# Powers of the table parameters as wide products and wide Exp steps, two parameter sets copied on chip, and new allowances for the virtual clock of an S4D and MLP-mixer kernel

## The chip, the cores and the metric

The kernel runs on one core of a Trainium2 chip. The metric is the device time of one execution in microseconds (us). Five engines matter here, each with its own instruction queue that is worked off strictly in order: PE (TensorE, with its weight loads shown apart as PEld), DVE (VectorE), ACT (ScalarE), POOL (GpSimd) and SP (SyncE, which only issues transfers). Instructions of different engines wait for each other through semaphores.

## What is computed

For a sequence of 2048 tokens with 576 channels the output is `x + s * g`:

```python
x = A_u
xn = _layernorm(x, axis=-1)
s = _A_ref(xn, ...)                  # S4D: a long convolution per channel
g = _silu(_B_ref(xn, ...))           # MLP mixer
return x + s * g

# _A_ref
dt = exp(log_dt); A = -exp(log_A_real) + 1j * A_imag
C = (C_real + 1j * C_imag) * dt[:, None]
P = exp((A * dt[:, None])[:, :, None] * pos)     # 576 x 128 x 2048
K = 2.0 * einsum("dn,dnl->dl", C, P).real
y = irfft(rfft(u, 2L) * rfft(K, 2L))[:L] + u * D_skip

# _B_ref
h = gelu(layernorm(x) @ w1 + b1)     # w1: 576 x 4608
return h @ w2 + b2                   # w2: 4608 x 576
```

## The kernel before, in words

**The main work is the MLP on PE.** It is done with each factor split in a high and a low part, and three products are added. The 4608 hidden units are taken in 12 groups of 3 x 128, the tokens in blocks of 512, two blocks to a half of the sequence. One group of weights on one block of tokens is called a *slot*; there are 48. A slot has eleven positions on PE: three blocks of layer 1 (line 621, 14 matmuls of 128x512 each, written to the PSUM tiles `mxa` and `mxb` in turn), then eight pieces of layer 2 (line 684, 72 matmuls of 128x288). In some slots a *pair* of matmuls (line 604) takes over rows that would else need one matmul more in two of the three blocks, which then have 13.

Behind each layer-1 block runs a hidden chain: ACT applies gelu (line 657, tile `h`) and rounds it to the high part `hh` (line 660); DVE subtracts to get the low part `hl` (line 663). Layer 2 multiplies `hh` with the high and low weights and `hl` with the high weights, so PE needs `hl` shortly after it begins with that block's part of layer 2. DVE also adds the pieces of layer 2 to `acc` (line 694), and ACT (574) and DVE (571) split the next weights.

**The S4D part runs as guests between these positions.** The kernel K is a sum over 128 modes. For each set of 16 channels there is a *table* (`tables(b)`, b from 0 to 35): DVE and ACT turn the set's parameters `par` into the tile `w` (phase 919 and 922, whole 925, frac 928, fold 931, Sin 936 and 938, magnitudes 944, weighing 953 to 959), and a PE guest `kg` (line 998, 64 matmuls, mean shape 32x64) sums over the modes. Further PE guests do the transforms of the convolution: x1 (1110), k1 (1141), s2 (1169), inv (1212), i1 (1238), for six chunks of 96 channels. A guest may ride inside another one (`ride`).

**The parameters come in four packs of 144 channels.** `params()` computes phases and magnitudes for all 576 channels on DVE and ACT (lines 822 to 860), in slots 1 to 5. Then `pack(i)` fills a buffer of 144 channels x 30 columns (`A` in the profile): 24 Exp instructions of 128x144 on ACT (line 878, one column each, `exp(-m * nrm)` for powers m of 1 to 7, 8 to 56, 64 to 448 and 512 to 1536), copies of the other columns on DVE (871 to 874), one product that puts the amplitude on the three last columns (881). POOL then stores the buffer to `par_s` in DRAM (887); the buffer is free for the next pack when that transfer has read it. `load_par(b)` (900, POOL) brings the 30 columns of each table's 16 channels back, two buffers deep.

**The order of all engines is written by a virtual clock.** The class `Order` (line 52) keeps a time for each engine. Work comes as lines of steps, each with an engine, an assumed duration, and marks it needs or sets. `take` adds the duration and the signal's delay `LAT`; while `shared` is set, DVE work that starts beside POOL work is counted longer by a factor. `advance` picks at each point the step that can start first; urgent chains (the hidden chains, the sums) have due times set by `hidden_by`, with an allowance `GAP`, from `LEN`, the assumed durations of PE's positions. Other work is only taken ahead of an urgent step where by the clock it ends before that step is due. `pe_turns` puts a guest on PE when by the clock its data will have been there for a margin (the -0.4); `END`, `EDGE`, `ALONE` and `DUE` spread the guests over the run. Each step is then tied to the one before it on its engine (`pin`), so the chip follows the written order, whatever its real times are. An assumed duration costs nothing by itself: it only decides the order.

## Time and profile before

| what | value |
|---|---|
| median of 3 runs | 1099.28 us (1099.13 to 1102.08) |
| profiled execution | 1098.31 us |
| its span (first to last instruction) | 1096.5 us |
| mean granted TensorE clock | 0.998 |
| PE busy | 1087.4 us (99%), 11445 matmuls |
| DVE busy | 891.3 us (81%) |
| ACT busy | 726.1 us (66%) |
| POOL busy | 184.1 us (17%) |
| mean DMA throughput | 126 GB/s |

The profiled execution's own time is 1.8 us more than its span. The span begins with the first instruction recorded and ends with the last. Rows of the trace give the start, the duration, engine, line and operation, written tile and read tiles; in brackets stands the idle time of the engine just before, and what ended it. Consecutive matmuls overlap in the pipeline, so what one costs is read from the distance between starts.

### The profile page before, as it was taken

The page shows a single profiled execution, that of the slowest core. Times are in us where ns is not written, and L with a number is a line of the kernel's source. Part 1 is how long each engine was busy: PE and PEld are TensorE (multiplying, and loading weights), DVE is VectorE, ACT ScalarE, POOL GpSimd, SP SyncE. Part 2 cuts the span into 40 slices and gives each one's busy share as a digit, 9 for nine tenths or more (in the row PEclk, how much of TensorE's full clock was granted, in tenths as well). Part 3 has the DMA queues.
Part 4 walks back from the last instruction along what each step waited for, and adds up shares of the span by engine and source line. Part 5 has one row for each costly group of instructions (what it writes and reads, how often), then busy time and mean ns, then how long its engine had stood idle before and what let it go on. Part 6 is the DMA issues. An engine that isn't in the chain of part 4 may idle for free.

```text
span 1096.5 us, 27039 instructions
## 1 busy us (share of the span) xinstructions
PE 1087.4 (99%) x11445; PEld 953.8 (87%) x11445; DVE 891.3 (81%) x1298; ACT 726.1 (66%) x1109; POOL 184.1 (17%) x255
## 2 busy tenths in 40 slices
PE   9999999999999999999999999999999999999997
PEld 7989899899888898888988888888888888888896
DVE  7798667889998879889899888997979887856356
ACT  6585699778666674777766848676685757435233
POOL 4566210153020100001100000000001021101130
PEclk9999999999999999999999999999999999999999
DMA  8746764626354152355623216133252434455454
GB/s 235 231 149 152 235 239 144 175 82 155 114 165 128 45 110 68 100 115 143 154 66 100 77 56 141 34 121 86 62 124 52 141 91 131 129 152 165 122 159 94
DMA packets 139649, 138.22 MB, mean 126 GB/s; under 512 B 88952, under 2 KB 105016, under 8 KB 138952
## 3 DMA queue, kind: packets, MB, share of 16 engines
q1 hardware_dynamic: 124664, 85.49, 29.2%
q0 software_dynamic: 14384, 50.27, 14.6%
q8 instruction: 89, 1.46, 0.5%
q10 hardware_dynamic: 480, 0.74, 0.3%
q14 instruction: 32, 0.26, 0.1%
HBM read 102.17 MB, written 36.63 MB: 127 GB/s over the span
## 4 chain that ended last, share of the span: by engine, by line
PE 94%; DVE 3%; DMA 1%; ACT 1%; SPq 1%; issue 0%; ACTq 0%; DVEq 0%
PE mxb L684 20%; PE mxa L684 20%; PE mxa L621 20%; PE mxb L621 19%; PE cv L1169 3%; PE cv L998 3%; PE cv L1212 2%; PE cv L1238 2%; PE cv L1141 1%; PE cv L1110 1%; DMA acc<-in_A_u_dram 0%; PE mxa L636 0%; PE mxb L604 0%; DMA raw<-in_B_w_dram 0%; PE cv L504 0%
## 5 line engine op out<-in xcount | busy, mean ns | idle before, releaser
L663 DVE TENSOR_TENSOR hl<-h,hh 128x512 fp32r<-128x512 f32 x144 | 98.6, 688 | 100.6 <-ACT hh L660 99.7
L684 PE MATMUL mxb<-w2h,hh 128*128 128x288 f32 x576 | 170.9, 297 | 0.0
L684 PE MATMUL mxb<-w2h,hl 128*128 128x288 f32 x576 | 170.3, 296 | 0.5 <-DVE hl L663 0.5
L684 PE MATMUL mxa<-w2h,hh 128*128 128x288 f32 x573 | 170.5, 298 | 0.0
L684 PE MATMUL mxb<-w2l,hh 128*128 128x288 f32 x576 | 169.5, 294 | 0.0
L684 PE MATMUL mxa<-w2h,hl 128*128 128x288 f32 x573 | 169.2, 295 | 0.0
L684 PE MATMUL mxa<-w2l,hh 128*128 128x288 f32 x573 | 168.6, 294 | 0.0
L657 ACT ACTIVATE h<-mxa,b1t 128x512 f32<-128x512 f32 x73 | 50.0, 687 | 99.0 <-PE mxa L621 97.2
L684 PEld LDWEIGHTS mxa<-w2h,hh 128*128 128x128 f32 x573 | 107.6, 188 | 6.0 <-issue 3.0
L684 PEld LDWEIGHTS mxb<-w2h,hh 128*128 128x128 f32 x576 | 108.2, 188 | 4.2 <-issue 2.0
L684 PEld LDWEIGHTS mxb<-w2l,hh 128*128 128x128 f32 x576 | 108.2, 188 | 0.8
L684 PEld LDWEIGHTS mxb<-w2h,hl 128*128 128x128 f32 x576 | 108.1, 188 | 0.7 <-DVE hl L663 0.7
L684 PEld LDWEIGHTS mxa<-w2l,hh 128*128 128x128 f32 x573 | 107.6, 188 | 0.6
L684 PEld LDWEIGHTS mxa<-w2h,hl 128*128 128x128 f32 x573 | 107.5, 188 | 0.0
L657 ACT ACTIVATE h<-mxb,b1t 128x512 f32<-128x512 f32 x71 | 48.8, 688 | 70.6 <-PE mxb L621 68.2
L900 POOL DMA_DIRECT2D par<-par_s x36 | 27.8, 773 | 400.2 <-DVE mg L944 357.3
L660 ACT ACTIVATE hh<-h 128x512 fp32r<-128x512 f32 x144 | 90.7, 631 | 3.7
L694 DVE TENSOR_TENSOR acc<-mxa,acc 128x576 f32<-128x576 f32 x87 | 65.3, 751 | 28.2 <-PE mxa L684 28.0
L694 DVE TENSOR_TENSOR acc<-mxb,acc 128x576 f32<-128x576 f32 x88 | 66.0, 750 | 18.3 <-PE mxb L684 18.1
L621 PE MATMUL mxa<-XH,w1h 128*128 128x512 f32 x284 | 79.3, 401 | 0.0
L621 PE MATMUL mxb<-XH,w1h 128*128 128x512 f32 x280 | 77.7, 399 | 0.0
L621 PE MATMUL mxa<-XL,w1h 128*128 128x512 f32 x284 | 76.2, 390 | 0.0
(266 smaller groups left out, 2481.1 us busy)
## 6 DMA issues: line engine op xcount, KB each, us to landing
raw<-in_B_w_dram SPq DMA_DIRECT2D x72, 288.0 KB, 3.3
raw<-in_B_w_dram SPq DMA_DIRECT2D x96, 192.0 KB, 3.5
par_s<-A POOLq DMA_DIRECT2D x4, 2160.0 KB, 8.1
par<-par_s POOLq DMA_DIRECT2D x36, 240.0 KB, 3.7
f2t<-f2q SPq DMA_DIRECT2D x24, 256.0 KB, 3.5
g2t<-g2p SPq DMA_DIRECT2D x24, 256.0 KB, 4.2
bias<-XR SPq DMA_DIRECT2D x42, 128.0 KB, 3.5
raw<-in_B_w_dram SPq DMA_DIRECT2D x48, 96.0 KB, 3.9
```

The costliest lines, as they stand in the source:

```text
L621: nc.tensor.matmul(q, a, b, start=j == 0 and i not in BEGUN, stop=j == len(ops) - 1, skip_group_check=True)
L657: nc.scalar.activation(t, q, AF.Gelu_apprx_tanh, bias=b1t[:, k:k + 1], scale=1.0)
L660: LAST[0] = nc.scalar.activation(hh[:, i], t, AF.Copy)
L663: nc.vector.tensor_sub(hl[:, i], t, hh[:, i].bitcast(F32))
L684: nc.tensor.matmul(q[:, dh, :288], a[:, i, c], b[:, i, d], start=i == 0 and k == 0 and not alone, stop=i == G - 1 and k == 2)
L694: nc.vector.tensor_add(o, q[:, dh:dh + n, :288], b)
L900: nc.gpsimd.dma_start(PAR[b].rearrange("p (g i) k -> p g (i k)", g=4), dram(par_s, (b // 3 * 48 + b % 3 * 4) * NPAR, [[D * NPAR, P], [12 * ...
L998: nc.tensor.matmul(q[32 * g:32 * g + 32, i // 2, i % 2 * 64:i % 2 * 64 + 64], U[:, ri, 4 * g + i, :], v[:, ri, 4 * g + i, :], start=ri == ...
L1110: nc.tensor.matmul(Q[24 * v][:, e], FP[0][r, f, 0], x[r, 12 * e:12 * e + 12], start=n == 0, stop=n == 2, skip_group_check=True)
L1169: nc.tensor.matmul(Q[i][32 * q:32 * q + 32, f, ri::2], m[r, 4 * i + q, 32 * ri:32 * ri + 32], A2[r, 4 * p + 2 * i + q // 2, :, :, q % 2], ...
L1212: nc.tensor.matmul(QI[q // 2][64 * f:64 * f + 64, q % 2, i], MAT["g2t", p + i // 2][r, i % 2, f, ri], YS[p + i // 2][0][r, i % 2, ri, f], ...
L1238: nc.tensor.matmul(Q[h][64 * y:64 * y + 64, t], g1t.rearrange("p a e -> p (a e)"), A2[:, k:k + 2, 1].rearrange("p i d r -> p i r d"), star ...
```

## The change

It has three parts. Nothing of the MLP's or the convolution's arithmetic is altered.

**Powers.** A small tile `em` (28 exponents) is made once by four tiny DVE instructions. In each pack, DVE multiplies `nrm` with `em` for 36 channels x 28 columns at a time (four products of 1008 elements per partition, new line 885), and ACT applies Exp in place to the same 1008 elements (four instructions, new line 889) in place of 24 instructions of 144. The memset and one of the three column copies go; the amplitude product takes four columns instead of three (new line 892). Since the products write the whole buffer on DVE, the first product of a pack waits for the store of the pack before. The products of pack 1 also come after the copies of the next part.

**Two tables' parameters.** For tables 0 and 1, `par` is no longer stored to DRAM and loaded back; DVE copies it from the buffer after pack 0 is complete (`copy_par`, new line 911, 128x480, twice).

**Allowances.** Almost all assumed durations and margins of the virtual clock get new values, and one new rule keeps a guest x1 from starting when less than 4.03 us of assumed PE time is left in the slot.

```diff
-    LAT = 0.2
+    LAT = 0.1894
...
         if eng == "DVE" and self.shared and start < self.t["POOL"] - 0.4:
-            dur *= 1.1
+            dur *= 1.0065
...
-        ex = [(E1 + k, k) for k in range(1, 8)] + [(E8 + k, 8 * k) for k in range(1, 8)]
-        ex += [(E64 + k, 64 * k) for k in range(1, 8)] + [(E512 + k, 512 * k) for k in range(1, 4)]
+        em = sb.tile([P, NPAR - E1], F32, name="em")
+
+        def exponents():
+            for a, k, m in ((E1, 8, 1.0), (E8, 8, 8.0), (E64, 8, 64.0), (E512, 4, 512.0)):
+                V.tensor_scalar(em[:, a - E1:a - E1 + k], tv[:, :k], m, None, op0=OP.mult)
+        early.append(step("DVE", 0.35, exponents, need=["tv"]))
 
         def pack(i):
             s = slice(i * PK, (i + 1) * PK)
 
             def columns():
-                if i == 0:
-                    V.memset(pt[:, :, E1:E1 + 17:8], 1.0)
                 V.tensor_copy(pt[:, :, 0], th[:, s])
                 V.tensor_copy(pt[:, :, 1], ph[:, s])
-                V.tensor_copy(pt[:, :, E512], cr[:, s])
+
+            n = PK // 4
+
+            def scaled(p):
+                r = slice(i * PK + p * n, i * PK + p * n + n)
+                V.tensor_mul(pt[:, p * n:p * n + n, E1:], bc(nrm[:, r], 2, NPAR - E1), bc(em, 1, n))
 
             def powers(p):
-                for k, m in ex[6 * p:6 * p + 6]:
-                    A.activation(pt[:, :, k], nrm[:, s], AF.Exp, scale=-float(m))
+                t = pt[:, p * n:p * n + n, E1:]
+                A.activation(t, t, AF.Exp, scale=-1.0)
 
             def rest():
-                V.tensor_mul(pt[:, :, E512 + 1:], pt[:, :, E512 + 1:], bc(cr[:, s], 2, 3))
+                V.tensor_mul(pt[:, :, E512:], pt[:, :, E512:], bc(cr[:, s], 2, 4))
             for p in range(4):
-                early.append(step("ACT", 1.85, lambda p=p: powers(p), tbl="exp", late=0.0,
-                                  need=() if i else [("xn", b) for b in range(4, 8)]))
-            early.append(step("DVE", 0.6 if i else 1.1, columns, need=["polar"]))
-            early.append(step("DVE", 0.65, rest))
+                early.append(step("DVE", dve(n * (NPAR - E1)), lambda p=p: scaled(p),
+                                  need=PARC if i == 1 else [("xn", b) for b in range(4, 8)]))
+            for p in range(4):
+                early.append(step("ACT", act(n * (NPAR - E1)) + 0.1, lambda p=p: powers(p), tbl="exp", late=0.0))
+            early.append(step("DVE", 0.45, columns, need=["polar"]))
+            early.append(step("DVE", dve(4 * PK) + 0.05, rest, mark=("rest", i)))
...
+    def copy_par(b):
+        PAR[b] = sb.tile([P, SB, NPAR], F32, name="par", bufs=2)
+        pt = A2F[:, PT0:PT0 + PK * NPAR].rearrange("p (d k) -> p d k", d=PK)
+        nc.vector.tensor_copy(PAR[b].rearrange("p (g i) k -> p g i k", g=4),
+                              pt[:, :48].rearrange("p (g j) k -> p g j k", g=4)[:, :, 4 * b:4 * b + 4])
...
-            if any(m not in od.marks for m in need) or max([kl["ready"]] + [od.marks[m] for m in need]) > od.t["PE"] - 0.4:
+            if any(m not in od.marks for m in need) or max([kl["ready"]] + [od.marks[m] for m in need]) > od.t["PE"] - 0.2128:
...
-    END = 1000.0
+    END = 960.4921
-    EDGE = 0.2, 0.6
-    ALONE, DUE = 20.0, (160.0, 950.0)
+    EDGE = 0.4961, 0.4684
+    ALONE, DUE = 31.1001, (127.7614, 950.0)
...
-                if h is None or h[0]["eng"] != "PE" or h[1] > od.t["PE"] + (0.3 if x is nl else -0.4):
+                if h is None or h[0]["eng"] != "PE" or h[1] > od.t["PE"] + (0.3 if x is nl else -0.234):
+                    break
+                if x is c1 and h[0]["mark"][0] == "x1" and edge is None and not any_time and sum(LEN[at[0] + 1:]) < 4.03:
                     break
...
-    GAP = 0.17
+    GAP = 0.2168
...
-                    od.urgent.append((od.t["PE"], [step("ACT", 0.67, a, tbl="gelu", by=by[0]),
-                                                   step("ACT", 0.6, b, by=by[1]),
+                    od.urgent.append((od.t["PE"], [step("ACT", 0.7, a, tbl="gelu", by=by[0]),
+                                                   step("ACT", 0.6134, b, by=by[1]),
```

The other new values: `LEN` of layer 2 from 0.132 to 0.1343 for a matmul and `L1` from 14 x 0.2315 to 14 x 0.2308; assumed durations of the guests x1, s2, inv, i1, kg from 1.5, 1.75, 2.15, 3.05, 1.03 to 1.417, 1.779, 2.0456, 3.2187, 1.0243; the allowance for the load of `par` from 10 (first six tables) and 4.5 to 6.4064 and 5.4203; for the loads of the final combination from 13 to 8.1292.

What this does to the order is shown at three places. The first is DVE in slot 2 (the third slot, 53 to 73 us before). `h_...` are the outputs of gelu of the slot's three blocks, `row` a normalized token block, `st` and `mv` the statistics of token blocks, `w2l` the low part of weights, `A_83` the parameter buffer. Before:

```order
L571 TENSOR_TENSOR w2l<-raw,w2h 128x576 x3
L832 TENSOR_TENSOR kt<-kt,pr 128x576
L444 TENSOR_SCALAR row<-w,mv,rs 128x576 x3
L663 TENSOR_TENSOR hl<-h_700,hh 128x512
L411 BN_STATS st<-w 128x6 x2
L413 BN_AGGR mv<-st 128x2
L663 TENSOR_TENSOR hl<-h_735,hh 128x512
L411 BN_STATS st<-w 128x6 x2
L413 BN_AGGR mv<-st 128x2
L411 BN_STATS st<-w 128x6
L663 TENSOR_TENSOR hl<-h_772,hh 128x512
```

The same place now:

```order
L571 TENSOR_TENSOR w2l<-raw,w2h 128x576 x3
L836 TENSOR_TENSOR kt<-kt,pr 128x576
L885 TENSOR_TENSOR A_83<-A_83,em 128x36x28 x2
L663 TENSOR_TENSOR hl<-h_701,hh 128x512
L885 TENSOR_TENSOR A_83<-A_83,em 128x36x28
L663 TENSOR_TENSOR hl<-h_738,hh 128x512
L885 TENSOR_TENSOR A_83<-A_83,em 128x36x28
L444 TENSOR_SCALAR row<-w,mv,rs 128x576 x2
L663 TENSOR_TENSOR hl<-h_759,hh 128x512
```

The four products of pack 0 now stand between the hidden chains' `hl`, and the statistics have moved behind them.

The second place is DVE in slot 5 (111 to 130 us before), where pack 0 is complete. Before, the columns of pack 0 are filled just ahead of it (lines 871 to 881), and the three `hl` stand alone:

```order
L871 MEMSET A_83 128x144x3
L872 COPY A_83<-A_83 128x144
L873 COPY A_83<-A_83 128x144
L874 COPY A_83<-xc 128x144
L881 TENSOR_TENSOR A_83<-A_83,xc 128x144x3
L694 TENSOR_TENSOR acc<-mxa,acc 128x576
L694 TENSOR_TENSOR acc<-mxb,acc 128x576
L663 TENSOR_TENSOR hl<-h_1306,hh 128x512
L663 TENSOR_TENSOR hl<-h_1328,hh 128x512
L663 TENSOR_TENSOR hl<-h_1351,hh 128x512
```

Now, from the first on-chip copy of parameters on (new lines 938, 941, 947 and 963 are the old 919, 922, 928 and 944):

```order
L911 COPY par<-A_83 128x480
L694 TENSOR_TENSOR acc<-mxb,acc 128x576
L911 COPY par<-A_83 128x480
L938 TENSOR_TENSOR w<-par,tv 128x16x65
L941 TENSOR_TENSOR w<-w,par 128x16x32
L663 TENSOR_TENSOR hl<-h_1278,hh 128x512
L963 TENSOR_TENSOR mg<-par 128x16x64
L947 TENSOR_TENSOR w<-w 128x16x65
L663 TENSOR_TENSOR hl<-h_1297,hh 128x512
L885 TENSOR_TENSOR A_83<-A_83,em 128x36x28
L963 TENSOR_TENSOR mg<-par 128x16x32
L663 TENSOR_TENSOR hl<-h_1327,hh 128x512
```

Table 0 has moved here from slot 6, and the first product of pack 1, which waits for the store of pack 0, now stands ahead of the slot's third `hl`.

The third place is PE at the first guest `kg`. Before, it stands in slot 8, between its second and third layer-1 block:

```order
L621 MATMUL mxa<-XR,w1s 128x512
L998 MATMUL cv<-w 32x64 x32
L621 MATMUL mxb<-XH,w1h 128x512 x4
L621 MATMUL mxb<-XL,w1h 128x512 x4
L621 MATMUL mxb<-XH,w1l 128x512 x4
```

Now it stands two slots earlier, in slot 6, behind all three layer-1 blocks and ahead of layer 2:

```order
L621 MATMUL mxb<-XR,w1r 128x512
L621 MATMUL mxb<-XR,w1s 128x512
L1020 MATMUL cv<-w 32x64 x32
L684 MATMUL mxa<-w2h,hh 128x288
L684 MATMUL mxa<-w2l,hh 128x288
L684 MATMUL mxa<-w2h,hl 128x288
```

Up to there PE's rows are the same in both kernels; from there to about 1000 us the guests stand at other places between the same blocks, and so do the steps of DVE and ACT that serve them. On POOL the store of pack 0 now stands directly behind the last store of normalized tokens (455), ahead of the loads of constants (273 to 280).

More of the change, by code (lines that the diff above doesn't have):

```diff
@@ L1117, in x1 @@
                 c0 = 48 * i + d0
[L1118 removed]
+                add("DVE", 0.8979, lambda d0=d0, c0=c0: nc.vector.transpose(
                     A2[:, :, 0, c0:c0 + 24].rearrange("p k d r -> p d k r"), Q[d0]), cv=-1)
@@ L1249, in i1 @@
                 add("ACT", act(8 * CH), lambda h=h: store(h), cv=-1, mark=("st", c) if h else None)
-        four.append(step(None, 5.0 if c else 12.5, lambda: load(0), mark=("xl", c, 0),
+        four.append(step(None, 6.6146 if c else 12.5, lambda: load(0), mark=("xl", c, 0),
                          need=[("xn", b) for b in range(NT)] + [("pack", D // PK - 1)]))
@@ L1470, in mixer_kernel @@
     tl["steps"].append(step(None, 14.0, load_tv, at=30.0))
-    tl["steps"].append(step("DVE", 0.15, scale_tv))
+    tl["steps"].append(step("DVE", 0.15, scale_tv, mark="tv"))
     norm_lines(8)
```

30 lines of the change are left out of this document (19 added, 11 removed).

## The prediction

> **What bounds the kernel now.** I read the page's busy times first, then the table of stretches, then the waits of PE, and last the neighbourhood of the one wait that PE shows.
>
> ```profile
> PE 1087.4 (99%) x11445; PEld 953.8 (87%) x11445; DVE 891.3 (81%) x1298; ACT 726.1 (66%) x1109; POOL 184.1 (17%) x255
> PE 94%; DVE 3%; DMA 1%; ACT 1%; SPq 1%; issue 0%; ACTq 0%; DVEq 0%
> ...
> 31.00:110.00 79.00, 79.00 (x481) 72.33 (x480) 67.53 (x114) 54.11 (x93) 49.54 (x45) 1.00 0.58 174
> 110.00:150.00 40.00, 40.00 (x241) 36.53 (x241) 23.89 (x53) 31.08 (x66) 7.59 (x14) 1.00 0.73 244
> 255.00:400.00 145.00, 145.00 (x1749) 125.74 (x1748) 128.62 (x170) 103.11 (x141) 15.47 (x23) 1.00 0.43 123
> 550.00:700.00 150.00, 149.51 (x1797) 129.77 (x1798) 133.46 (x178) 105.27 (x143) 7.04 (x9) 1.00 0.30 81
> 850.00:1000.00 150.00, 150.00 (x1883) 129.74 (x1889) 113.39 (x164) 87.58 (x138) 21.45 (x38) 1.00 0.46 133
> ...
> 1087.25 1.20 PE mxa L684 x9
> ...
> 1091.74 0.46 DVE w L782
> ```
>
> The first two rows are the busy times and the chain that ended last: PE carries 94% of it. In the stretches (start:end, length, busy time of PE, PEld, DVE, ACT, POOL, then clock, DMA share, GB/s) PE is busy for the whole of 79, 40 and 145 us, at a clock of 1.00; only one stretch shows less, 149.51 of 150. The last two rows are from the chain's end: after PE's last matmuls some 8 us of ACT and DVE work follow, which the change does not touch. So the time is PE's work in a row, and another engine's work counts only where it makes PE wait. The one wait after the start:
>
> ```profile
> PE mxb L684 <- DVE hl L663: 0.5, 1, 0.5
> ...
> 568.39 0.29 PE L684 MATMUL mxb<-w2l,hh 128*128 128x288 f32 x1
> 569.17 0.40 PE L684 MATMUL mxb<-w2h,hl 128*128 128x288 f32 x1 [0.49 <-DVE hl L663]
> 569.41 0.29 PE L684 MATMUL mxb<-w2h,hh 128*128 128x288 f32 x1
> ...
> 565.70 1.23 DVE L919 TENSOR_TENSOR w<-par,tv 128x1040 f32<-128x1040 f32 x1
> 566.96 0.69 DVE L922 TENSOR_TENSOR w<-w,par 128x512 f32<-128x512 f32 x1
> 567.57 0.95 DVE L1090 TENSOR_TENSOR ys<-kt,pr 128x768 fp32r<-128x768 f32 x1
> 568.44 0.68 DVE L663 TENSOR_TENSOR hl<-h,hh 128x512 fp32r<-128x512 f32 x1
> ```
>
> Three table and guest steps (565.70 to 568.44) stood ahead of `hl` on DVE. The starts 568.39 to 569.41 take 1.02 us where two distances of 0.13 (0.26) would do: the wait cost 0.76 us. That is my price of one stall.
>
> **The change, part by part. PE's own work.** PE issues the same products in another order, with two pairs more: by the code 32 pair matmuls become 36 and 1942 layer-1 matmuls 1938.
>
> ```profile
> 171.62 3.17 PE mxa L621 x14
> 174.79 1.03 PE cv L998 x64
> 175.82 3.40 PE mxb L621 x14
> ...
> 250.94 0.43 PE mxb L604 x2
> ```
>
> A layer-1 matmul costs 3.17/14 = 0.226, a pair 0.43: 2 x 0.43 - 4 x 0.226 = -0.05 us. The block behind a guest costs 3.40 instead of 3.17, so an interruption costs 0.23; counting the guests' runs between MLP positions in the two orders gives 74 in each, so 0. The first `kg` now stands two slots earlier, which moves 1.03 us of PE work and removes none. The last three slots are free of guests in both, so the tail stays.
>
> **Powers on ACT and DVE.**
>
> ```profile
> L878 ACT ACTIVATE A<-A 128x144 f32<-128x144 f32 x96 | 28.3, 510 | 0.1
> L878 ACT ACT_TABLE_LOAD x5 | 6.4, 1283 | 0.1
> L938 ACT ACTIVATE w<-w 128x1040 f32<-128x1040 f32 x36 | 39.1, 1086 | 0.1
> L953 DVE TENSOR_TENSOR w<-w,mg 128x1024 f32<-128x1024 f32 x36 | 43.8, 1217 | 4.3 <-ACT w L938 4.3
> L881 DVE TENSOR_TENSOR A<-A,xc 128x432 f32<-128x432 f32 x4 | 2.5, 617 | 1.3 <-ACT A L878 1.3
> ```
>
> ACT loses 28.3 us and gains 16 Exps of 1008, nearest the 1086 ns row: 17.4. The order has four more table loads, at 1.283 each: 5.1. ACT gets 5.8 us less. DVE gains 16 products nearest the 1217 ns row, 19.5 us; four `rest` widen by a third of 617 ns (+0.8), a memset and four copies go (-1.6), two copies of 480 elements come (about +1.1 from `rest`). DVE goes from 891 to about 911 us. All of it lies beside PE as long as it is not ahead of an `hl` that is due. Up to 150 us PE's stretches leave DVE 11 of 79 and 16 of 40 us idle, which is the cover. Two places are tight.
>
> *Slot 2.* Four products now stand among the hidden chains:
>
> ```profile
> 54.19 0.75 DVE L694 TENSOR_TENSOR acc<-mxa,bias 128x576 f32<-128x576 f32 x1
> 54.86 0.19 DVE L439 RECIPROCAL rs<-rs 128x8 f32<-128x8 f32 x1
> 55.58 2.09 DVE L571 TENSOR_TENSOR w2l<-raw,w2h 128x576 fp32r<-128x576 f32 x3
> 57.58 1.22 DVE L832 TENSOR_TENSOR kt<-kt,pr 128x576 f32<-128x576 f32 x1
> 58.72 1.40 DVE L444 TENSOR_SCALAR row<-w,mv,rs 128x576 f32<-128x576 f32 x2
> ...
> 55.84 3.97 POOL L454 TENSOR_SCALAR w<-w,mv,rs 128x576 f32<-128x576 f32 x1 [9.48 <-ACT w2h L574]
> 64.30 2.29 POOL L454 TENSOR_SCALAR w<-w,mv,rs 128x576 f32<-128x576 f32 x1
> ...
> 65.82 0.31 PE L684 MATMUL mxa<-w2h,hl 128*128 128x288 f32 x1
> ```
>
> By starts, from 54.86: exponents about 0.35 (estimate: four instructions no longer than the reciprocal's 0.19), reciprocal 0.22, weights 2.00, `kt` 0.67 (alone) to 1.14 (as here): 58.1 to 58.6. Two products of 1.14, `hl` 0.6, product, `hl`, product: 63.9 to 64.3. Two `row` steps, 1.4, then the third `hl`, 0.6 to 0.7: 65.8 to 66.4. PE takes it at 65.82. Stall 0 to 0.6; I take 0.2, nearer the undisturbed end, since only one POOL step in this stretch reached 3.97.
>
> *Slot 5.* The first product of pack 1 waits for the store of pack 0, and behind it in DVE's queue stands the third `hl`, for which PE waits.
>
> ```profile
> 118.85 0.69 DVE L663 TENSOR_TENSOR hl<-h,hh 128x512 fp32r<-128x512 f32 x1 [2.48 <-ACT hh L660]
> 122.02 0.69 DVE L663 TENSOR_TENSOR hl<-h,hh 128x512 fp32r<-128x512 f32 x1 [2.48 <-ACT hh L660]
> ...
> 123.07 0.29 PE L684 MATMUL mxb<-w2h,hl 128*128 128x288 f32 x1
> ...
> DMA to landing us min/median/max: 6.9/8.1/9.9
> ...
> DMA to landing us min/median/max: 3.0/3.7/10.9
> ```
>
> The last two rows are the stores of packs (line 887) and the loads of `par` (900). In the new order `rest` of pack 0 ends at about 110.7 (a sum `acc` at 106.34, three products and another sum of 0.67 by the distance 54.19 to 54.86, two copies of 0.14, and 0.75), so the store, issued at once, lands at 117.6, 118.8 or 120.6. The product needs 1.14, the magnitudes behind it 0.60: `hl` starts at 122.02 as before unless the store lands after 120.3. Stall 0 at the median; at 9.9 the `hl` starts 0.3 late, against 0.36 of slack. I take 0.05, with ends 0 and 1.1 (a landing as long as the longest of `par`, 10.9). The Trainium skill, page "SBUF — State Buffer", section "SBUF: two separate sides", says that a transfer issued from GpSimd's queue cannot have its descriptors written while DVE runs an fp32 copy in SBUF. No row of before has such a transfer beside such a copy; by this rule the two copies of parameters, right behind `rest`, would make the store about 1 us later, and the sum would be 1 us more at a landing of 9.9 and nothing more at 8.1.
>
> **The other moves.** On POOL the store of pack 0 now stands ahead of the constants' loads, which moves them some 20 us later; their first use on DVE moves one slot later too, so 0. Table 0 and 1 save a load of 3.0 to 10.9 us each and begin a slot earlier; nothing on PE waited for them, so 0. The new numbers re-sort guests from 140 to 1000 us. The stall of 0.76 at 568 belongs to an old neighbourhood and goes; the new order has DVE work exceeding PE's time in six slots, against seven before, by a sum of durations per slot, so I expect one to two new ones like it: 1.1 us, with ends 0 and 4.6 (one in each of the six).
>
> **Sum.** 1098.31 - 0.05 - 0.76 + 0.2 + 0.05 + 1.1 = 1098.85 for a profiled execution. The median of the runs stands 0.97 above the profiled one, so 1099.8. What this kernel's measurement can tell from no change is about 0.3%, 3.3 us: faster means below 1096.0, slower above 1102.6.
>
> **Rivals.** *New stalls add up (slower).* The clock's margins shrink: a guest is placed 0.23 instead of 0.4 after its data, DVE beside POOL counts 1.0065 instead of 1.1, and 72 layer-2 matmuls count 9.67 instead of 9.50 us, so about 0.17 us more DVE and ACT work is admitted to each slot than the chip's PE leaves. For it: DVE is at 89% from 255 to 400 and from 550 to 700, and the one stall came from a full DVE. Against it: it happened once in 37 slots with guests, and the gelu steps' allowances grew. From six stalls on top of the sum it decides (six x 0.76 = 4.6: 1104.4).
>
> *The lock (slower).* `L832` took 1.22 beside POOL's 3.97, where `L694` with the same shape takes 0.75, so DVE and POOL do disturb each other in slot 2. If each product waited for a whole POOL step, two or three of 2.29 would fall ahead of the third `hl`: 4.6 to 6.9 more, 1104.4 to 1106.7; it decides from two. Against it: among 144 `hl`, also of two SBUF inputs, the longest is 905 ns against 691.
>
> ```profile
> L663 DVE TENSOR_TENSOR hl<-h,hh x144: 626/691/905, 21.7 to 1081.0; 128x512 fp32r<-128x512 f32 x144
> ```
>
> The same section of the Trainium skill calls the port that DVE and GpSimd share an exclusive lock, also for a DVE operation with two SBUF inputs against a GpSimd operation that reads SBUF: the loser waits for all of it. By that rule this rival holds; the trace agrees only in part, since POOL is stretched there more than DVE.
>
> *A store or load is late (slower).* DVE waits in order for the store in slot 5, and for table 2's `par`. It needs a store of 13 us, against 9.9 as the longest: 123.7 + 0.6 for `hl`, about 3 us: 1102.9.
>
> *PE gets faster.* If guests behind three full blocks fit better, at most the 0.23 of some interruptions and the 0.76 go: 15 of the 74 would be needed for 3.4 us, 1095.9. The fixed starts (3.17 in all stages) speak against it.
>
> *The change does nothing for PE.* ACT's 66% never bounded it; then the time is 1099.3, inside the forecast's band.
>
> **Chances.** My forecast, within 0.3%: 0.70, and the change without effect 0.02. Stalls add up 0.16, a late transfer 0.05, the lock 0.03: slower 0.24. PE faster 0.04. The range goes from 1097.5 (the old stall gone, no new one, at the profiled level: 1098.31 - 0.81) to 1104.4 (six stalls); it leaves out the lock's upper part, PE faster and part of the stalls, under 0.2. The forecast's own range is 1097.5 to 1102.6.
>
> **What would show it.** Right: PE busy over the whole of each stretch after 31 us, waits of PE for `hl` of 0.5 to 2 us in all, the third `hl` of slot 2 ending near 66.0, the first product of pack 1 starting before 120.6, ACT's Exps of the powers at about 1.09 and products at 1.2. Wrong: PE waits of more than 4 us in all, on `hl` or on guests' data; or the products at 2 us and more beside POOL's steps.

## The result, and the profile after

The changed kernel takes 1104.57 us (median of 6 runs, 1103.37 to 1105.29), the kernel before 1099.39 us (6 runs beside it, 1098.14 to 1102.08). The ratio is 1.0044, with a 95% interval of 1.0031 to 1.0057: slower by 4.8 us, and by more than the 0.3% that I had called the limit. The profiled execution took 1104.64 us, 6.3 more than the one of before. It lies on the side to which I gave 0.24. By the median it is 0.2 us above the upper end of my range; by the ratio, put on the 1099.28 from which the range was worked out, it is 1104.1 and 0.3 inside.

The page of the kernel after (busy times and the chain that ended last), then four of the same stretches as before, then PE's waits for `hl`:

```profile
PE 1089.3 (99%) x11445; PEld 952.7 (86%) x11445; DVE 909.4 (82%) x1315; ACT 720.4 (65%) x1033; POOL 180.8 (16%) x253
...
PE 87%; DVE 5%; DMA 3%; SPq 2%; ACT 2%; issue 1%; ACTq 0%; DVEq 0%
```

```profile
31.00:110.00 79.00, 76.34 (x448) 68.24 (x447) 68.11 (x112) 51.84 (x74) 37.82 (x26) 1.00 0.55 175
110.00:150.00 40.00, 38.11 (x282) 34.17 (x282) 34.60 (x48) 24.55 (x32) 16.09 (x30) 1.00 0.56 180
...
255.00:400.00 145.00, 145.00 (x1762) 125.56 (x1760) 129.97 (x174) 105.03 (x141) 26.78 (x43) 1.00 0.46 125
...
550.00:700.00 150.00, 149.47 (x1756) 129.90 (x1755) 131.32 (x177) 102.06 (x141) 6.29 (x8) 1.00 0.34 89
```

```profile
PE mxb L684 <- DVE hl L663: 3.0, 2, 1.9
PE mxa L684 <- DVE hl L663: 2.0, 4, 1.2
```

The chain has less of PE in it than before (87% instead of 94%), and PE is 2.7 and 1.9 us short of the first two stretches, which before were full. From 150 us on, where the guests were sorted anew, PE is as busy as before to within 0.2 us a stretch. So nearly all of the loss is made before 150 us. The waits of PE there, in the row of the instruction that waited:

```profile
47.65 0.40 PE L684 MATMUL mxb<-w2h,hl 128*128 128x288 f32 x1 [1.09 <-DVE hl L663]
...
103.46 0.40 PE L684 MATMUL mxa<-w2h,hl 128*128 128x288 f32 x1 [0.24 <-DVE hl L663]
105.29 0.40 PE L684 MATMUL mxa<-w2h,hl 128*128 128x288 f32 x1 [1.17 <-DVE hl L663]
107.69 0.40 PE L684 MATMUL mxa<-w2h,hl 128*128 128x288 f32 x1 [0.16 <-DVE hl L663]
...
128.95 0.40 PE L684 MATMUL mxb<-w2h,hl 128*128 128x288 f32 x1 [1.89 <-DVE hl L663]
```

By starts of PE's positions against their usual length (a stall is what one takes beyond it, counted from 0.3 us on) these cost 1.37 us in slot 1, 1.94 and 0.44 in slot 4, and 2.17 in slot 5. At 551 to 555 us stalls of 0.71 and 0.36 have taken the place of the 0.76 at 568, and one of 0.32 stands at 975. That is 7.31 us against 0.76, 6.55 more, where the two executions differ by 6.33.

**Slot 4.** DVE, the first time in the changed kernel, then POOL in the same microseconds:

```profile
98.94 0.99 DVE L855 TENSOR_SCALAR A<-kt 128x576 f32<-128x576 f32 x1
99.97 1.95 DVE L857 RECIPROCAL A<-A 128x288 f32<-128x288 f32 x1
101.84 1.56 DVE L663 TENSOR_TENSOR hl<-h,hh 128x512 fp32r<-128x512 f32 x1
103.33 1.31 DVE L444 TENSOR_SCALAR row<-w,mv,rs 128x576 f32<-128x576 f32 x1
104.56 0.67 DVE L663 TENSOR_TENSOR hl<-h,hh 128x512 fp32r<-128x512 f32 x1
...
97.96 3.13 POOL L454 TENSOR_SCALAR w<-w,mv,rs 128x576 f32<-128x576 f32 x1
...
102.03 2.29 POOL L454 TENSOR_SCALAR w<-w,mv,rs 128x576 f32<-128x576 f32 x1
```

The normalizations of the last token blocks (`row`, 444) stood in slots 2 and 3 before; the products have taken their place in slot 2, and four of them with their POOL halves (454) now fall into slot 4, where the reciprocals of 1.95 us stand. The `hl` for which PE waits comes after three of them, the weights and a reciprocal, and then takes 1.56 us, more than twice its usual 0.69. The slot by itself, in the kernel before and in the kernel after:

```profile
91.80:110.90 19.10, 19.10 (x117) 17.45 (x116) 16.89 (x25) 6.98 (x10) 11.25 (x22) 1.00 0.48 105
```

```profile
93.00:114.70 21.70, 20.13 (x117) 17.46 (x115) 20.83 (x28) 9.51 (x15) 12.37 (x8) 1.00 0.50 167
```

DVE's 20.83 us (third engine column) are more than the 19.1 us that PE's slot takes without a stall; before they were 16.89. In the kernel before, the first `hl` of this slot took 0.63:

```profile
98.99 0.63 DVE L663 TENSOR_TENSOR hl<-h,hh 128x512 fp32r<-128x512 f32 x1
```

**Slot 5.** The second `hl`, the first product of pack 1 and the third `hl`; then the stores of packs (line 900 of the kernel after):

```profile
122.67 0.69 DVE L663 TENSOR_TENSOR hl<-h,hh 128x512 fp32r<-128x512 f32 x1 [0.19 <-ACT hh L660]
126.49 1.21 DVE L885 TENSOR_TENSOR A<-A,em 128x1008 f32<-128x1008 f32 x1 [3.12 <-DMA par_s<-A]
...
128.22 0.68 DVE L663 TENSOR_TENSOR hl<-h,hh 128x512 fp32r<-128x512 f32 x1
...
DMA to landing us min/median/max: 7.3/7.9/11.3
```

The store of pack 0 is the one of 11.3 us. DVE stood 3.12 us idle for it, with the third `hl` behind, which started at 128.22.

**Slot 1.** DVE in the kernel after, then in the kernel before:

```profile
41.05 0.46 DVE L411 BATCH_NORM_STATS2 st<-w 128x6 f32<-128x288 f32 x1 [5.37 <-DMA w<-in_A_u_dram]
41.43 0.67 DVE L663 TENSOR_TENSOR hl<-h,hh 128x512 fp32r<-128x512 f32 x1
...
46.92 0.68 DVE L663 TENSOR_TENSOR hl<-h,hh 128x512 fp32r<-128x512 f32 x1
```

```profile
39.37 0.72 DVE L663 TENSOR_TENSOR hl<-h,hh 128x512 fp32r<-128x512 f32 x1 [3.27 <-ACT hh L660]
40.05 0.82 DVE L411 BATCH_NORM_STATS2 st<-w 128x6 f32<-128x288 f32 x2
...
45.71 0.69 DVE L663 TENSOR_TENSOR hl<-h,hh 128x512 fp32r<-128x512 f32 x1 [0.19 <-ACT hh L660]
```

One statistics step (`st`), which waits for a load of x rows, has moved ahead of the slot's first `hl`; up to the third `hl` the rest of DVE's order is the same. ACT had `hh` ready at 38.96, but the load landed only at 41.03 (40.03 before), and the first `hl` and all behind it waited for it.

### The profile page after: what moved, and what is told of

Read it like the earlier page. It is cut to its first block, busy times and chain, and to the rows that moved or that the text cites. A ratio compares the mean times of both kernels' runs of the same rounds, so it can differ in the third digit from the quotient of the medians.

```text
span 1102.9 us, 26963 instructions
## 1 busy us (share of the span) xinstructions
PE 1089.3 (99%) x11445; PEld 952.7 (86%) x11445; DVE 909.4 (82%) x1315; ACT 720.4 (65%) x1033; POOL 180.8 (16%) x253
## 4 chain that ended last, share of the span: by engine, by line
PE 87%; DVE 5%; DMA 3%; SPq 2%; ACT 2%; issue 1%; ACTq 0%; DVEq 0%
PE mxb L684 19%; PE mxa L684 19%; PE mxa L621 18%; PE mxb L621 18%; PE cv L1020 3%; PE cv L1191 3%; PE cv L1234 2%; PE cv L1260 2%; PE cv L1163 1%; PE cv L1132 1%; DMA par_s<-A 1%; SPq L816 1%; DVE hl L663 1%; DMA w<-in_A_u_dram 1%; DMA f2t<-f2q 1%
## 5 line engine op out<-in xcount | busy, mean ns | idle before, releaser
L657 ACT ACTIVATE h<-mxb,b1t 128x512 f32<-128x512 f32 x71 | 48.8, 688 | 65.9 <-PE mxb L621 61.5
L621 PE MATMUL mxa<-XH,w1l 128*128 128x512 f32 x284 | 76.1, 390 | 0.0
```

Of the source, the lines that this page charges most:

```text
L621: nc.tensor.matmul(q, a, b, start=j == 0 and i not in BEGUN, stop=j == len(ops) - 1, skip_group_check=True)
L657: nc.scalar.activation(t, q, AF.Gelu_apprx_tanh, bias=b1t[:, k:k + 1], scale=1.0)
```

## The experiments

Theory A: the time is lost at a few places where DVE, in its order, is late with an `hl`; those of slots 4 and 5 come from the new powers. Theory B: the new allowances cost it, all over the run. "Ratio" is against the kernel before, run beside on the same chip.

**Old allowances with the new powers.**

```diff
-    LAT = 0.1894
+    LAT = 0.2
...
-    GAP = 0.2168
+    GAP = 0.17
...
```

(all of them, and the rule for x1 off)

> The new powers and the two on-chip copies, with every allowance of the virtual clock as before (and without the new rule for x1). Theory A (the time is lost in slots 4 and 5, by DVE work that the new products displace or that waits for the store of pack 0, whatever the allowances): in slot 4 the first hl still stands behind three row steps, the weights and a reciprocal, and in slot 5 a product of pack 1 still stands ahead of the third hl; waits of PE for hl of 2 to 5 us before 150 us, time 1102 to 1104.5. Theory B (the new allowances cost the time, all over the run): 1098.5 to 1100.

Measured: 1117.45 us, ratio 1.0178 (1.0165 to 1.0191). Both theories missed it. Before 150 us there are stalls of 0.71, 0.44 and 0.60; two other things cost more. At 478 us DVE waits for a transfer, and PE behind it for a sum:

```profile
485.29 0.71 DVE L479 STREAM_TRANSPOSE row<-row 128x512 f32<-128x512 f32 x1 [6.39 <-DMA row<-y_s]
...
489.62 0.61 PE L684 MATMUL mxb<-w2h,hh 128*128 128x288 f32 x1 [6.26 <-DVE acc L694]
```

And the span ends 12.6 us after the last matmul instead of the 5.8 of the changed kernel, with stores of the final combination on POOL. So the new powers under the old allowances give a much worse order: taken together with the powers the new allowances save time, some 14 us by the ratios. Which one of them does was not tried. In slot 1 the first `hl` stands ahead of the statistics again, and there is no stall, though the load of x rows landed at 40.93, about as late as in the kernel after.

**New allowances with the old powers** (the kernel before with the reverse of that edit).

```diff
-    LAT = 0.2
+    LAT = 0.1894
...
-    GAP = 0.17
+    GAP = 0.2168
...
```

> The kernel before with only the new allowances and the rule for x1: 24 Exps of 144 per pack, and the parameters of all tables through DRAM. Theory A: no product stands ahead of an hl in slots 2, 4 and 5, so PE waits less than 1.5 us in all, 1098 to 1100. Theory B: 1103 to 1105.

Measured: 1100.18 us, ratio 1.0012 (1.0004 to 1.0021); stalls of 0.41, 1.04 and 1.00. By the ratio 1.3 us slower, not 4.8: theory B falls as an account of the whole, though 1.3 of the 4.8 can be theirs, and A's 1098 to 1100 is missed by 0.2. The statistics step stands ahead of slot 1's first `hl` here too. So that move belongs to the new allowances and not to the powers; the load landed at 39.98 in this profile, and the move cost nothing.

**Powers behind the normalizations, and longer allowance for the store.**

```diff
-                                  need=PARC if i == 1 else [("xn", b) for b in range(4, 8)]))
+                                  need=PARC if i == 1 else [("xn", b) for b in range(4, 16)]))
...
-            early.append(step(None, 8.0, lambda: None, mark=("pack", i)))
+            early.append(step(None, 8.0 if i else 13.0, lambda: None, mark=("pack", i)))
```

> The changed kernel, but the products of pack 0 may only begin when all 16 token blocks are normalized (they move from slot 2 to the end of slot 4), and the clock allows 13 instead of 8 us for the store of pack 0. Theory A: in slot 4 the three hl stand as in the kernel before, in slot 5 nothing waits for the store; PE waits under 1.5 us after 31 us, time 1098 to 1100. Theory B: all new allowances are still there, so 1103 to 1105.

Measured: 1101.77 us, ratio 1.0030 (1.0018 to 1.0042). Slots 4 and 5 have no stall, as A says; but the order behind has others, of 0.3 to 0.85 us at 402, 524, 569, 682, 685 and 904 us, and one of 0.48 in slot 1, 3.6 in all. The two places were the cause there, and the time still came out 1.8 above A's range, because a new order has new places.

**The store of pack 0 in four transfers.**

```diff
-            early.append(step("POOL", 0.8, lambda: nc.gpsimd.dma_start(par_s[:, s, :], pt)))
+            early.append(step("POOL", 0.8, lambda: [nc.gpsimd.dma_start(par_s[:, i * PK + a:i * PK + b, :], pt[:, a:b]) for a, b in (((0, 36), (36, 72), (72, 108), (108, 144)) if i == 0 else ((0, 144),))]))
```

> The changed kernel with the store of pack 0 cut into four transfers of 36 channels; the order of DVE, ACT and PE stays as it is, POOL has three issues more. The first product of pack 1 writes only the first 36 channels, so it waits only for the first transfer. Theory A: that lands in 3 to 7 us instead of 11.3, the wait of 3.1 us in slot 5 goes, PE's stall of 2.15 there goes to under 0.5, and the time falls by 1.7 to 2.2 to 1102.4 to 1103. Rival (the store ended late for what stands behind it in POOL's queue, not for its size): the first transfer also lands after 10 us or more, and the time stays at 1104 to 1105.

Measured: 1101.14 us, ratio 1.0033 (1.0022 to 1.0045), where the changed kernel has 1.0044 to 1.0054. The stores' landing, which include the four parts:

```profile
DMA to landing us min/median/max: 3.1/7.3/8.9
```

The first part lands after 3.1 us, and no stall is left in slot 5. The median is below the 1102.4 to 1103 that I expected. The store as a whole is not quicker: its last part, with the constants' loads behind it, lands 10.7 us after the first was issued. Its profiled execution (1104.52) had stalls of 3.9 us in slot 1; four of the seven runs lie at 1100.2 to 1101.2, three at 1103.0 to 1104.5.

**The changed kernel again, without its first reciprocal, and without POOL's last normalizations.** These three and the next ran beside each other.

> The changed kernel once more, unaltered, for a second trace and as the base of the three beside it. Theory A (two stalls that belong to the new order, one that comes and goes): slot 4 (PE's first hl, 1.9 us) and slot 5 (the product behind the store of pack 0, 2.2 us, store landing after more than 10 us) show again within 0.5 us; the stall of 1.4 us in slot 1, where the loads of x rows came late, is between 0 and 4 us and may be absent; 1102.5 to 1104.5. Rival (all three are chance of the transfers): slot 5 or slot 4 shows less than half.

Measured: 1103.41 us, ratio 1.0054 (1.0041 to 1.0067). Waits of PE:

```profile
103.93 0.40 PE L684 MATMUL mxa<-w2h,hl 128*128 128x288 f32 x1 [1.17 <-DVE hl L663]
...
127.28 0.40 PE L684 MATMUL mxb<-w2h,hl 128*128 128x288 f32 x1 [1.56 <-DVE hl L663]
```

Slot 4 costs 1.96 and 0.44 again, slot 5 1.84 (the store lands after 11.0 us), slot 1 nothing: its order is that of the first trace, but the load landed at 40.24. The first two came with the order both times; the third did not, and a late load seems to be needed for it.

```diff
-            add("DVE", 1.9, lambda h=h: V.reciprocal(ci[:, h], ci[:, h]))
+            add("DVE", 1.9, lambda h=h: h is H[1] and V.reciprocal(ci[:, h], ci[:, h]))
```

> The changed kernel without the reciprocal of the first half of the amplitudes (line 857, one of two instructions of 1.95 us; the values it made are left out, the order of everything else stays). Theory A: the first hl of slot 4 stands at the end of a full DVE queue, so it comes 1.9 us earlier, PE's stall there falls from 1.9 to under 0.4, the time by 1.5 to 2.2 against the changed kernel. Rival (hl is late because ACT or a weight load is): the stall keeps over 1.2 us.

Measured: 1102.23 us, ratio 1.0033 (1.0020 to 1.0046). The same two rows of slot 4, now with DVE idle ahead of `hl`:

```profile
100.40 0.69 DVE L663 TENSOR_TENSOR hl<-h,hh 128x512 fp32r<-128x512 f32 x1 [0.17 <-ACT hh L660]
101.01 0.69 DVE L444 TENSOR_SCALAR row<-w,mv,rs 128x576 f32<-128x576 f32 x1
```

Both stalls of slot 4 are gone, slot 5 keeps 2.10. The median is 1.2 us under the changed kernel's, less than the 1.5 I had as the least; its profiled execution had 1.75 us of stalls in slot 1.

```diff
-            nc.gpsimd.tensor_scalar(x, x, mv[:, t, 0:1], rs[:, 0, t:t + 1], op0=OP.subtract, op1=OP.mult)
+            if b0 + t < 12: nc.gpsimd.tensor_scalar(x, x, mv[:, t, 0:1], rs[:, 0, t:t + 1], op0=OP.subtract, op1=OP.mult)
```

> The changed kernel without POOL's four normalizations of the last token blocks (line 454 for blocks 12 to 15; their rows go to DRAM unnormalized, so their part of the convolution's input is another). They run at 94.7 to 107.6 us, beside slot 4. Theory C (POOL slows DVE in slot 4): the first hl there takes 0.7 instead of 1.56, the row step behind it 0.6 instead of 1.3, and PE's stall falls from 1.9 to 0.4 to 1.1. Rival (only POOL is stretched by the two engines' meeting, as in the kernel before): hl stays over 1.2 us and the stall over 1.6.

Measured: 1103.34 us, ratio 1.0045 (1.0031 to 1.0058). The first `hl` of slot 4 and the row step behind it, with the reciprocal back ahead of them and nothing on POOL; and PE's wait in slot 5:

```profile
100.10 0.63 DVE L663 TENSOR_TENSOR hl<-h,hh 128x512 fp32r<-128x512 f32 x1
100.64 0.57 DVE L444 TENSOR_SCALAR row<-w,mv,rs 128x576 f32<-128x576 f32 x1
...
126.69 0.40 PE L684 MATMUL mxb<-w2h,hl 128*128 128x288 f32 x1 [3.06 <-DVE hl L663]
```

`hl` falls from 1.56 to 0.63, the row step from 1.31 to 0.57, and slot 4 has no stall, less than the 0.4 I expected to stay. So POOL's work beside DVE's is what turns a full slot into a late one: without it the same DVE queue is in time. The time stays all the same (1103.41 for the changed kernel beside it). Slot 5 gives back 1.5 of the 2.4 us: the store, issued 1.8 us earlier, lands after 12.3, and the stall there is 3.34 instead of 1.84. The rest is within the spread of these few runs (1101.88 to 1104.6).

**Both places mended by the clock.** The store in four, and the clock told that a reciprocal takes longer:

```diff
-            add("DVE", 1.9, lambda h=h: V.reciprocal(ci[:, h], ci[:, h]))
+            add("DVE", 4.0, lambda h=h: V.reciprocal(ci[:, h], ci[:, h]))
```

> The changed kernel with the store of pack 0 in four transfers and the virtual clock told that a reciprocal of 288 takes 4.0 instead of 1.9 us, so that in slot 4 it stands behind the three hl. Theory A: no stall over 0.5 us in slots 4 and 5, the rest of the run is sorted anew; 1098.5 to 1101, at best equal to the kernel before, since PE's own work is the same. Theory B (the allowances cost it over the whole run): over 1102.

Measured: 1105.89 us, ratio 1.0075 (1.0061 to 1.0089). Slots 4 and 5 are free of stalls, and the rest of the order has become worse; two of PE's waits:

```profile
PE cv L1020 <- DVE w L978: 2.5, 1, 2.5
PE mxa L684 <- DVE acc L694: 1.5, 1, 1.5
```

One of 2.5 us is for a table's last step, at 200 us. Theory A held for the places and failed for the time. The time is in theory B's range, but this edit sorted the whole run anew, so it can't tell the allowances from any other new order.

**Both places mended with all else in its place.** The store in four, and the two reciprocals of slot 4 issued later without the clock's knowledge:

```diff
+    BACK = []
...
             nc.vector.tensor_sub(hl[:, i], t, hh[:, i].bitcast(F32))
+            if BACK and BACK[0][0] == i + 1:
+                BACK.pop(0)[1]()
...
-            add("DVE", 1.9, lambda h=h: V.reciprocal(ci[:, h], ci[:, h]))
+            add("DVE", 1.9, lambda h=h: BACK.append((2 if h is H[0] else 3, lambda: V.reciprocal(ci[:, h], ci[:, h]))))
```

> The changed kernel with only the two places mended and every other row where it is: the store of pack 0 in four transfers, and the two reciprocals of slot 4 each issued behind an hl instead of ahead of one (the first behind the second hl, the second behind the third). Theory A (the two places are the loss that belongs to the order): no stall over 0.5 us in slots 4 and 5, only those of 0.7 and 0.4 at 550 us stay, time within 1.5 us of the kernel before, 1097.5 to 1099.7, apart from runs with the stall in slot 1. Theory B (the loss is spread over the re-sorted run, and mending two places only moves it): 1101 or more.

Measured: 1100.98 us, ratio 1.0015 (1.0006 to 1.0024). PE's wait in slot 4 is another now:

```profile
108.58 0.40 PE L687 MATMUL mxa<-w2h,hh 128*128 128x288 f32 x1 [1.33 <-DVE acc L697]
```

PE does not wait for an `hl` there any more but, 1.5 us, for the first sum, which stands behind the second reciprocal and two products. Slot 5 is clean. 1.96 us above the kernel before (1099.02): 1.3 more than A's upper end, at the edge of B's 1101, and 1.5 of it is this stall.

**And once more, with the sums ahead.** The second reciprocal and one product go behind the first sum, two products behind the second:

```diff
-            add("DVE", 1.9, lambda h=h: V.reciprocal(ci[:, h], ci[:, h]))
-        add("DVE", d, lambda: V.tensor_mul(T[1], T[1], cr))
-        add("DVE", d, lambda: V.tensor_sub(T[1], T[3], T[1]))
-        add("DVE", d, lambda: V.tensor_mul(T[1], T[1], ci))
+            add("DVE", 1.9, lambda h=h: BACK["hl" if h is H[0] else 1].append(lambda: V.reciprocal(ci[:, h], ci[:, h])))
+        add("DVE", d, lambda: BACK[1].append(lambda: V.tensor_mul(T[1], T[1], cr)))
+        add("DVE", d, lambda: BACK[2].append(lambda: V.tensor_sub(T[1], T[3], T[1])))
+        add("DVE", d, lambda: BACK[2].append(lambda: V.tensor_mul(T[1], T[1], ci)))
```

> As the kernel mended in place, which kept a stall of 1.5 us in slot 4 because the second reciprocal and two products still stood ahead of the first sum (acc): now the second reciprocal and one product stand behind the first sum, two more products behind the second. Theory A (the loss is the sum of the stalls): no stall over 0.5 us in slots 4 and 5, only the 0.7 and 0.4 near 550 us stay against 0.8 in the kernel before; 0 to 0.7 us above the kernel before of the same chip (ratio 1.0000 to 1.0007). Theory B (something else in the re-sorted order costs time): 1.5 us or more above it, with no stall to show for it.

Measured: 1102.33 us, ratio 1.0033 (1.0021 to 1.0045). The wait has moved on, to the first layer-1 block of slot 5:

```profile
114.16 1.20 PE L622 MATMUL mxa<-XH,w1h 128*128 128x512 f32 x4 [1.73 <-DVE acc L697]
```

That is 2.01 us of stall, for the third sum of slot 4; 0.69 in slot 1 and 1.04 at 973 us (PE waits 0.9 there for a transfer, `f2t`) come to it. So my expectation failed: what is moved from one wait comes up at the next. The slot is not simply too full, since DVE now stands idle in it for 0.18 and 0.47 us ahead of two `hl` and for 1.10 us ahead of the first sum; the work that was moved comes too late behind these.

**What stands behind the store.** The constants' loads, which the new order issues on POOL right behind the store of pack 0, go to SP:

```diff
-            nc.gpsimd.dma_start(t[r], g1[64 * k + 32 * h:64 * k + 32 * h + 32, 32 * h:32 * h + 32])
+            nc.sync.dma_start(t[r], g1[64 * k + 32 * h:64 * k + 32 * h + 32, 32 * h:32 * h + 32])
...
```

> The changed kernel with the constants' loads (lines 273 to 280) issued by SP instead of POOL, so that nothing stands behind the store of pack 0 in POOL's queue. Theory D (the small transfers behind the store share its queue and delay its end): the store lands after 7 to 8.5 us instead of 11.0 to 12.3, the stall in slot 5 falls from 1.8 to 3.3 to under 0.5, time 1101 to 1102. Rival (the store is late for its own size or for other traffic): it lands after 10 us or more, time as the changed kernel, 1103 to 1104.5, or more if SP's weight loads now come late.

Measured: 1103.69 us, ratio 1.0042 (1.0029 to 1.0054). The stores:

```profile
DMA to landing us min/median/max: 7.3/7.9/8.3
```

The store of pack 0 is the 8.3, and slot 5 has no stall, with DVE's order unchanged. So the constants' loads did delay the store, as theory D has it. I had expected nothing behind the store in POOL's queue, and that is not so: POOL now issues four loads of `f2p` (512 KB each) and three of `kk` right behind it. In the kernel before, the same seven stood right behind that store, and it landed after 8.3 there too. So it matters which transfers follow. Whether the shared queue or the time does it stays open: of the 17 loads on SP, twelve were issued before the store and five while it was under way.

The time did not follow. Stalls of 0.53 and 0.96 us at 454 and 973 us came up, and the span ends 8.1 us after the last matmul instead of 5.8: 4.2 us after the last transfer has landed, where the kernel after needs 1.4. What it waits for there the trace does not show.

**The kernel before again.**

> The kernel before, unaltered, for a second trace. Its only stall after 31 us should be again the 0.76 at 568 us; whether the loads of x rows in slot 1 come late here too (a stall of 0 to 4 us at 44 to 49 us) is open: the order there is the same in both kernels, so I expect it as often as in the changed kernel's five traces, three of five.

Measured: 1098.4 us; stalls of 0.79 at 568 us and 0.35 at 545, none in slot 1. I had written that the order there is the same in both kernels; it is not. Here the first `hl` stands ahead of the statistics, as in the first trace of the kernel before.

**All profiled executions together.**

| kernel | profiled us | stalls after 31 us | difference |
|---|---|---|---|
| before, twice | 1098.31, 1098.40 | 0.76, 1.14 | 1097.6, 1097.3 |
| after, twice | 1104.64, 1103.08 | 7.31, 5.88 | 1097.3, 1097.2 |
| new allowances, old powers | 1099.68 | 2.45 | 1097.2 |
| powers behind the normalizations | 1101.13 | 3.59 | 1097.5 |
| store in four | 1104.52 | 6.78 | 1097.7 |
| no first reciprocal | 1103.69 | 6.17 | 1097.5 |
| no last POOL normalizations | 1102.29 | 4.40 | 1097.9 |
| both mended by the clock | 1109.19 | 10.75 | 1098.4 |
| mended in place, again | 1101.04, 1103.06 | 3.22, 4.81 | 1097.8, 1098.3 |
| constants on SP | 1104.75 | 4.93 | 1099.8 |
| old allowances, new powers | 1116.34 | 10.69 | 1105.7 |

What is left without the stalls is 1097.2 to 1098.4 us for all but the last two. These have a longer end: the span goes on for 4.2 and 5.7 us after the last landing, where it is 1.3 to 1.7 in the others. The last one also shows a granted clock of 0.83 from 480 to 500 us, around its stall of 6.4. So the loss is, to about 1 us, the sum of a few countable stalls. No kernel tried beats the one before.

## Where the prediction was right and where it was wrong

The forecast, no change within 0.3%, failed, and my sign of being wrong came: PE waits 5.0 us for `hl` in all, more than 4. The profiled execution came out 5.79 us above the 1098.85 of the sum. Slot 4 accounts for 2.38 of it, slot 5 for 2.12, slot 1 for 1.37 and the re-sorted stretch for 0.29, together 6.16. That the time lies at the upper end of the range is luck: that end stood for six new stalls of the re-sorting, and three small ones came.

- **PE bounds the kernel, and only stalls count: right.** The table shows it for twelve executions of ten kernels. PE's own work did not change (the -0.05 of the pairs is below what the differences can tell), and the rival that PE gets faster had no ground.
- **The prices of the new instructions: right.** The products measure 1.20 us (I took 1.217), the Exps 1.04 (1.086). ACT's busy time falls by 5.7 us (5.8 forecast), DVE's rises by 18.1 (about 20).
- **Slot 2: right in the number, in part by luck.** The third `hl`:

```profile
65.79 1.08 DVE L663 TENSOR_TENSOR hl<-h,hh 128x512 fp32r<-128x512 f32 x1 [0.15 <-ACT hh L660]
```

  It ends at 66.9, by a PE that runs 1.0 us later than before, so 65.9 by the old clock (66.0 forecast); the stall is 0.17 (0.2). But the products did not make it late. DVE was done with them in time and stood idle for 0.15 us until ACT had `hh`, where my sum has DVE late by itself; and `hl` took 1.08 beside a POOL step where I took 0.6 to 0.7. The two errors cancel.
- **The re-sorted stretch: right.** I took 1.1 us of new stalls for the 0.76 that went; 0.71, 0.36 and 0.32 came.
- **"Two places are tight": the step that failed.** I looked at slots 2 and 5, where the new instructions stand, and not at slot 4, where the work that they displaced came to stand. The order that I read shows the row steps there. By undisturbed durations slot 4 would have fitted: 20.83 us of DVE, less 0.53 for `L855` (0.46 before), 0.93 for the `hl` (0.63 without POOL) and 0.74 for the row step, is 18.6 of PE's 19.1. What I left out is that POOL's half of each normalization moves along and slows DVE; that the `hl` and the row step take their usual time without POOL's was shown by leaving its steps out. The slot cost 2.4 us, which is in no term of my sum.
- **Slot 5: right mechanism, wrong size.** The wait stood where I put it, with the `hl` behind it. I priced the store from the four rows of before (6.9 to 9.9) and took 0.05 with an upper end of 1.1 (1.0 by its own terms); it took 11.3, 11.0, 11.2 and 12.3 in four profiles, and the stall was 2.17. By my own rows a landing of 11.3 would give 1.4; the rest is that the store was issued at 115.14, some 0.7 us later by the old clock than the 110.7 of my sum. Before, the constants' loads were issued ahead of that store; in the new order they follow it at once in POOL's queue. I had read that move on POOL and charged it to the constants only. With them on SP the landing was 8.3, which is what this store took before.
- **The rule on copies and GpSimd's transfers** (the Trainium skill, page "SBUF — State Buffer", section "SBUF: two separate sides") would also have made the store late, but it is not what did: with the copies in their place and the constants on SP the store landed after 8.3 us, as it did before without copies, and POOL took 0.55 for the issue as always.
- **The lock as a rival: half right, in another slot.** DVE and POOL did disturb each other, at the price of 0.93 us for one `hl`. The rule of the Trainium skill (page "SBUF — State Buffer", section "SBUF: two separate sides"), that of a DVE operation with two SBUF inputs and a GpSimd operation that reads SBUF the one that starts second waits for all of the other, is not what the trace shows: that `hl` began before the POOL step, at 101.84 against 102.03, and ended at 103.40, while the POOL step ran to 104.32. I had set this rival aside because the longest of 144 `hl` before took 905 ns. Eleven of these met a POOL step, and ten of the eleven took 0.64 to 0.72; so meeting one is not enough, and from the rows of before I could not have told which `hl` would be slowed.
- **Slot 1, 1.37 us: in no term of my sum.** I took DVE's order ahead of slot 2 to be that of before, and it is not: the new allowances put a statistics step, which waits for a load, ahead of the first `hl`. Eleven profiles have this order, and six of them the stall (0.5 to 3.9 us); the three with the old order have none. In five of the six the load landed at 40.9 us or later, in the sixth a later load of x rows was late (44.1), and in the five without the stall it had landed by 40.6. With the old order and a load at 40.93 there was no stall. This points to the order, which lets a late load reach PE. But no run moved this step alone, and why the load is late in some executions is not shown.
- **The tail: it stayed, but I misread it.** After the last matmul of the kernel before come 6.4 us of span. ACT and DVE work takes about 2 of them; the rest is the last stores and the end, where I had read 8 us of work.
- **The chances.** Stalls adding up had 0.16 and a late store 0.05 apart from each other; they came together, 2.4 and 2.2 us, neither of which alone passes 3.3. I had a condition for each ("from six stalls", "a store of 13 us") and none for the sum of the two; neither condition was met, and the time was slower all the same.

## What to carry to other kernels

Where one engine is busy from end to end and the others follow a written order, an edit's price is not its instructions' but that of the late places it makes: look at the slots into which displaced work moves, with the other engines' share of that work, as closely as at those where the new instructions stand. A wait for a transfer in an in-order queue is priced with the transfers that will stand right behind it in the new order, not by the landings of the place it had before: one store took 8.3 us with some loads behind it and 11.0 to 12.3 with others. Compare the two orders instruction by instruction from the start, also where nothing was meant to change: one swapped pair in slot 1 stood ahead of stalls of up to 3.9 us. And when an order is made by a planner, mending one place through the planner's numbers makes new ones; to test a cause, move single instructions with the rest held.

## What was unexpected of the hardware

- Beside POOL's 128x576 step, DVE's `hl` took 1.56 us instead of 0.63, a `TENSOR_SCALAR` of 128x576 1.31 instead of 0.57. Yet most `hl` that met a POOL step kept their time: ten of eleven in the kernel before took 0.64 to 0.72. Which of the two engines is slowed does not follow from which began first. An `hl` that began 0.19 us ahead of the POOL step took 1.56 and left POOL its 2.29; another that began 0.25 us ahead (60.53 us, kernel before) took 0.68, and POOL's step 2.59. What decides it these rows do not show.
- A store of 2160 KB landed after 8.3 us with seven loads of `f2p` and `kk` right behind it on its queue, and after 11.0 to 12.3 when the constants' small loads were issued right behind it.
- The span went on after the last landing for 1.3 to 1.7 us in twelve profiles, for 4.2 in the one with seventeen more loads on SP, and for 5.7 in the one with the old allowances and the new powers. The cause is not known.
